# A planned attention and feed-forward kernel: single-row loads for batch 2, three more tiles transposed by DMA, and the sink values of later batches loaded already spread

## The chip, the cores and the metric

The kernel runs on one core of a Trainium2 chip. The metric is the device time of one execution in microseconds. Thirteen executions of the kernel before are on record; their median is 225.15 us. PE is the matrix engine, PEld its weight loads, DVE the vector engine, ACT the scalar engine, POOL the GpSimd engine and SP the engine that only issues DMAs and waits.

## The reference, cut to what matters

Attention with a window of 128 positions and four sink positions, for 4 batches, 8 heads, 768 positions and head width 64, is followed by a normalised two-layer feed-forward block with a residual.

```python
scores = scale * np.matmul(q, k.transpose(0, 1, 3, 2))
keep = is_sink | in_window            # key < 4, or 0 <= query - key < 128
a = softmax(np.where(keep, scores, -1e9))
attn = np.matmul(a, v)                # B, H, S, D
x = attn.transpose(0, 2, 1, 3).reshape(B, S, H * D)
xn = (x - mean) / np.sqrt(var + 1e-6) * g_ln
out = x + np.maximum(xn @ w_ch1, 0.0) @ w_ch2     # 512 -> 2048 -> 512
```

## The kernel before, in words

The 3072 positions are 24 tiles of 128, six to a batch: tile `t` is row block `r = t % 6` of batch `t // 6`. The tiles are collected into eight groups for the feed-forward part, of 2, 2, 2, 4, 4, 4, 4 and 2 tiles (`GROUPS`). So tiles 6 to 9 are group 3, and batch 2 is tiles 12 to 17.

The program is not written in its order. Each piece of work is an `Op` with the engines that may run it, an estimated duration on each, the pieces that it depends on, a key (its urgency) and the buffers that it takes or uses. `Plan.emit` walks a model of the engines, takes next what can start first (among nearly equal starts the lowest key), and emits the instructions in that order. It reserves PSUM itself: two double banks (`"pw"`, names `wide`) and four single banks (`"pm"`, names `single`). While the plan's clock stands under 26 us it also inserts filler matmuls on a constant tile (`spin`). On each engine the emitted order is final, so an instruction that has to wait holds up all that stand behind it on that engine. DMA queues count as engines in this: casting loads are issued from POOL, transposing DMAs and output stores from SP.

For one tile, `scores` multiplies q and k into double banks, ACT takes the exponential, and DVE or POOL clears what lies outside the window. `values` multiplies the result with v. Where it is `joined`, the values of tile `t - 1` are the first part of one PE piece with the scores of tile `t` and take two single banks; for the tiles of `ALONE` (6 to 9) the values are a PE piece of their own and take one double bank. `normalise` divides, takes mean and variance and centres the tile into a buffer `xn` (six of them), all on DVE. Then the tile has to be turned, with the model dimension on the partitions, into the buffer `xnt` of its group (three of those). Tiles from `DMA_TILE = 10` on are turned by a transposing DMA from SP (line 753). Tiles 0 to 9 are turned on PE by four transposes into a single bank (line 763) and copied out by DVE or ACT (line 766, which calls line 223 or 225).

The sinks are worked per batch in `sinks`. `mul_k` spreads the four sink keys, four small matmuls give the sink scores (line 534) and ACT takes their exponential. For the sink values, two matmuls with a selecting matrix copy the four sink rows of v to all partitions (`mm_v`, line 521), and two DVE multiplications with the mask `smask` keep those of each head (`mul_v`, line 527). In batches 1 to 3 `mm_v` takes a double bank.

`up` and `down` are the two matrix products of the feed-forward part (lines 787 and 827), with ACT or DVE taking the maximum with zero between them, and a DVE instruction and an SP store at the end of each tile. Their order is fixed by `mlp_order`: the three first groups all go up, then all go down, and from group 3 on each group goes up and then down. Attention of a tile has a key some 30 us of feed-forward work ahead of its group's place in that order, so the planner slips it in between.

Loads of batch 0, the weights, q and k of batch 1 and v of batch 1 are queued first, with at most seven casting loads outstanding. Then batch 2 is queued in one run: twelve loads of q and k, each of which is followed by a transposing DMA from SP (line 482), and later six of v. Batch 3 is queued row by row, each row once the scores of an earlier row of batch 2 have been taken.

Of the kernel before, what the change touches and what calls it, by code (L numbers as in the profile page):

```python
# [9 lines left out]
BF16 = mybir.dt.bfloat16  # L10
# [11 lines left out]
class Op:  # L22
    def __init__(self, engs, fn, deps, key, alloc, uses):
        self.engs, self.fn, self.key = engs, fn, key
        self.deps, self.alloc = [d for d in deps if d is not None], list(alloc)
        self.deps += [b.users[0] for b in uses if b.users]
        self.end = None
        for b in list(alloc) + list(uses):
            b.users.append(self)


# [132 lines left out]
def kernel(  # L164
# [12 lines left out]
    nc = tc.nc  # L177
# [16 lines left out]

    GROUPS = [2, 2, 2, 4, 4, 4, 4, 2]
    ALONE = (6, 7, 8, 9)
    NB0 = 3
# [51 lines left out]
    NEG_TILES = 3  # L249
    DMA_TILE = 10  # L250
    W2_FIRST = 3
# [71 lines left out]
    op({"POOL": 0.5}, const_sel, [begun], -499.4)  # L323
    sinks_done = op({"POOL": 0.9}, const_sinks, [begun], -440)


# [91 lines left out]
    def load_w(which, c, key, took=2.6):  # L418
# [8 lines left out]
        w_in[(which, c)] = load(0.85, took, go, key)  # L427


    prepped, kqb, turns = {}, {}, {}  # L430
# [67 lines left out]

    def sinks(b, key):

# [10 lines left out]

        vb = [Buf("pw", 0)] if b else [Buf("pm", 0), Buf("pm", 0)]

        def mm_v(_):
            if b:
                halves = [room_for(vb[0])[:, i] for i in range(2)]
            else:
                halves = [room_for(i) for i in vb]
            vb[0].t = halves
            for half in range(2):  # L520
                nc.tensor.matmul(halves[half][:, 0:4 * (D + 1)], lhsT=sel,
                                 rhs=vn_buf[b % 2][:, 0, 4 * half:4 * half + 4, 0:D + 1],
                                 start=True, stop=True, skip_group_check=True)

        def mul_v(_):
            for half in range(2):
                nc.vector.tensor_tensor(
                    vs[:, 4 * half:4 * half + 4], vb[0].t[half][:, 0:4 * (D + 1)].rearrange("p (h d) -> p h d", d=D + 1),
                    smask[:, 4 * half:4 * half + 4].unsqueeze(2).to_broadcast([128, 4, D + 1]), op=ALU.mult)

        def mm(_):
# [8 lines left out]

        o1 = op({"DVE": 0.2}, mul_k, ready(b, range(HP), 0, NS, 0, 0) + [sunk.get(b - 2), sinks_done, edone.get((RB * b, 0)) if b else None], key, (), [kb])
        ov = op({"PE": 0.22}, mm_v, [vcast[(b, 0)], sinks_done, ones_done] + ready(b, range(HP), 0, 0, 256, S), key, vb)
        vs_done[b] = op({"DVE": 0.8}, mul_v, [ov, vread.get((b - 2, RB - 1))], key, (), vb)
        o2 = op({"PE": 0.4}, mm, [o1] + ready(b, range(HP), 0, 0, 256, S), key, [pb], [kb])
        sunk[b] = op({"ACT": 0.6}, ex, [o2], key, [eb], [pb])

    ebuf = {}

    def scores(t, halves, key, lead=None):

# [13 lines left out]
        def mm(_):  # L564
            if lead:
                lead.fn(None)
            for pb, eb, part in zip(pbs, ebs, parts):
# [7 lines left out]
                for i, hp in enumerate([2 * half + i for half in part for i in range(2)]):  # L575
                    for h2 in range(2):
                        nc.tensor.matmul(pb.t[:, h2, i],  # L577
                                         lhsT=kb.t[64 * h2:64 * (h2 + 1), 1, hp, 128 * r:128 * (r + 1)],
                                         rhs=kb.t[64 * h2:64 * (h2 + 1), 0, hp, 128 * r:128 * r + n],
                                         start=not added, stop=True, skip_group_check=True)  # L580

        cost = 0.2 + 0.23 * n / 256 * len(halves) + (0.43 * len(halves) if added else 0.0)
        hps = [2 * half + i for half in halves for i in range(2)]
        deps = ready(b, hps, 128 * r, 128 * (r + 1), 128 * r, 128 * r + n) + [neg_done, edone.get((t - 1, 1)) if last else None]
        if lead:
            o0 = op({"PE": cost + lead.cost}, mm, deps + lead.deps, key, lead.alloc + pbs + ebs, [kb] + lead.uses)
            lead.rest(o0)
        else:
            o0 = op({"PE": cost}, mm, deps, key, pbs + ebs, [kb])

        for pb, eb, part in zip(pbs, ebs, parts):
# [25 lines left out]
            for half in part:  # L617
                edone[(t, half)] = o

    def weights_of(t, half, i, h2, lo):  # L620
# [6 lines left out]

    class Lead:
        pass

    def values(t, key, joined=False):

# [3 lines left out]
        vn, vs = vn_buf[b % 2], vs_buf[b % 2]  # L636
        banks = [Buf("pm", 0), Buf("pm", 0)] if joined else [Buf("pw", 0)]
        sums = []
# [9 lines left out]
        def mm(_):  # L648
            po = [room_for(i) for i in banks]
            po = po if joined else [po[0][:, i] for i in range(2)]  # L650
            sums[:] = [i[:, 0:4 * (D + 1)] for i in po]
# [30 lines left out]
        if joined:  # L682
            lead = Lead()
            lead.fn, lead.deps, lead.alloc, lead.uses, lead.cost = mm, deps, banks, uses, cost
            lead.rest = lambda o: normalise(t, key, o, banks, sums)
            return lead
        normalise(t, key, op({"PE": cost}, mm, deps, key, banks, uses), banks, sums)

    def normalise(t, key, o, banks, sums):
# [61 lines left out]

        if t >= DMA_TILE:
            o = op({"SP": 1.25}, lambda _: nc.sync.dma_start_transpose(room(), xnb[t].t), [o], key, alloc,
                   [xnb[t], xtb[g]])
            turned[t] = op({"XD": 0.4}, None, [o], key, (), [xnb[t], xtb[g]], 6.0 if t < 18 else 0.0)
            return
# [96 lines left out]
    def attention(t, key):  # L853

        alone = t - 1 in ALONE
        scores(t, (0, 1), key, None if alone or t == RB else values(t - 1, key, True))
        if alone:
            values(t - 1, key - 0.5)
        if t == NT - 1:
            values(t, key + 1.0)  # L860
# [27 lines left out]
    for r in range(RB):  # L888
        load_v(1, r, -430 + r)

    for b in range(B):
# [25 lines left out]
        if b == 1:  # L917
            for hp in range(HP):
                prep_runs(1, 0, hp, k0 - 12 + 3 * hp)
        else:  # L920

            for r in range(RB if b == 2 else 0):
                for x in range(2):
                    load_qk(b, x, r, k0 - 60 + r)
            for r in range(RB if b == 2 else 0):
                load_v(b, r, k0 - 50 + r, [prepped[(b, RB - 1, 1)]])
        for r in range(RB):
            if b == B - 2:

                t = RB * (b + 1) + r  # L930
                seen = [edone[(RB * b + r - 1, 0)]] if r else []
                for x in range(2):
                    load_qk(b + 1, x, r, akey(t) - 45, seen + [prepped[(b, RB - 1, 1)]])
                load_v(b + 1, r, akey(t) - 40, seen)
            attention(RB * b + r, akey(RB * b + r))
            if r == 1:
                sinks(b, akey(RB * b + 2) - 1)

# [53 lines left out]
```

## Time and profile before

| what | value |
|---|---|
| median of 13 executions | 225.15 us |
| shortest and longest of them | 224.54 and 1254.28 us |
| second longest | 225.8 us |
| the profiled execution | 1254.28 us |
| its span, first to last instruction | 1252.6 us |
| PE busy in that span | 1228.8 us |
| DVE, ACT, POOL busy | 116.0, 115.1, 85.6 us |

The profiled execution is the one that took 1254.28 us; the other twelve lie between 224.54 and 225.8 us. Its clock column shows 1.000 throughout, yet its matmuls are far too long for a time of 225 us. Durations on the other engines are those of single instructions and don't depend on PE. Read from the page, then, the order of all instructions, and the durations on DVE, ACT, POOL and the DMA queues; durations on PE have to be scaled before they can be set against 225.15 us.

### The profile page before, as it was taken

The page shows a single profiled execution, that of the slowest core. Times are in us where ns is not written, and L with a number is a line of the kernel's source. Part 1 is how long each engine was busy: PE and PEld are TensorE (multiplying, and loading weights), DVE is VectorE, ACT ScalarE, POOL GpSimd, SP SyncE. Part 2 cuts the span into 40 slices and gives each one's busy share as a digit, 9 for nine tenths or more (in the row PEclk, how much of TensorE's full clock was granted, in tenths as well). Part 3 has the DMA queues.
Part 4 walks back from the last instruction along what each step waited for, and adds up shares of the span by engine and source line. Part 5 has one row for each costly group of instructions (what it writes and reads, how often), then busy time and mean ns, then how long its engine had stood idle before and what let it go on. Part 6 is the DMA issues. An engine that isn't in the chain of part 4 may idle for free.

```text
span 1252.6 us, 4479 instructions
## 1 busy us (share of the span) xinstructions
PE 1228.8 (98%) x1805; PEld 427.3 (34%) x1826; DVE 116.0 (9%) x239; ACT 115.1 (9%) x159; POOL 85.6 (7%) x116
## 2 busy tenths in 40 slices
PE   9999999999999999999999999999999999999998
PEld 5445555623242322223332232322232322222433
DVE  1101000111110111111100100100000100000000
ACT  1211101110100111100011100011000011000000
POOL 5001040000030001010000000000000000000000
DMA  9024190001053004022100000000000000000000
GB/s 172 12 39 59 9 89 0 1 0 30 17 45 27 21 13 34 4 34 38 25 0 5 4 8 13 17 4 0 0 9 21 13 5 0 0 17 8 9 0 17
DMA packets 84774, 25.59 MB, mean 20 GB/s; under 512 B 74385, under 2 KB 81809, under 8 KB 84754
## 3 DMA queue, kind: packets, MB, share of 16 engines
q0 software_dynamic: 59392, 13.24, 12.0%
q1 hardware_dynamic: 24818, 11.67, 3.8%
q10 hardware_dynamic: 544, 0.39, 0.1%
q8 instruction: 14, 0.23, 0.1%
q14 instruction: 6, 0.05, 0.0%
HBM read 27.27 MB, written 6.29 MB: 27 GB/s over the span
## 4 chain that ended last, share of the span: by engine, by line
PE 98%; issue 2%; DVE 0%; DVEq 0%
PE single L787 40%; PE single L827 39%; PE wide L577 5%; PE single L237 2%; PE single L661 1%; PE wide L573 1%; PE wide L458 1%; PE single L458 1%; PE wide L661 1%; PE single L664 1%; PE single L763 1%; PE wide L664 1%; PE wide L644 1%; PE single L644 0%; PE single L867 0%
## 5 line engine op out<-in xcount | busy, mean ns | idle before, releaser
L787 PE MATMUL single<-xnt,w1s 128*128 128x256 bf16 (+1 forms) x505 | 505.1, 1363 | 6.6 <-issue 6.6
L827 PE MATMUL single<-w2s,h1t 128*128 128x512 bf16 x247 | 331.0, 1703 | 7.3 <-issue 7.3
L787 PEld LDWEIGHTS <-w1s 128*128 128x128 bf16 x512 | 157.6, 310 | 333.8 <-issue 333.2
L827 PE MATMUL single<-w2s,h1n 128*128 128x512 bf16 (+2 forms) x139 | 167.5, 1542 | 4.7 <-issue 4.7
L827 PEld LDWEIGHTS <-h1t 128*128 128x128 bf16 x256 | 78.2, 308 | 247.0 <-issue 247.0
L593 ACT ACTIVATE e<-wide 128x1024 bf16<-128x1024 f32 x44 | 45.0, 1024 | 371.1 <-PE wide L577 359.6
L827 PEld LDWEIGHTS <-h1n 128*128 128x128 bf16 x144 | 42.5, 303 | 104.6 <-issue 103.9
L840 DVE SCALAR_TENSOR_TENSOR ot<-single,rs,xt 128x512 f32<-128x512 f32 (+2 forms) x25 | 18.2, 729 | 542.5 <-PE single L827 523.2
L796 ACT ACTIVATE h1t<-single 128x512 bf16<-128x512 f32 x60 | 35.8, 597 | 327.9 <-PE single L787 312.1
L577 PE MATMUL wide<-qkt 64*128 64x256 bf16 (+1 forms) x192 | 62.9, 921 | 0.0
L605 POOL TENSOR_SCALAR_AFFINE_SELECT e<-e 128x512 bf16<-128x512 bf16 (+1 forms) x13 | 9.3, 716 | 662.3 <-ACT e L593 662.3
L661 PEld LDWEIGHTS <-e 128*128 128x128 bf16 x192 | 46.4, 254 | 22.0 <-issue 22.0
L664 PEld LDWEIGHTS <-e 128*128 128x128 bf16 x160 | 39.0, 249 | 16.8 <-issue 16.8
L796 ACT ACTIVATE h1n<-single 128x512 bf16<-128x512 f32 x30 | 17.9, 597 | 230.2 <-PE single L787 230.2
L661 PE MATMUL single<-vn,e 128*128 128x65 bf16 x104 | 35.4, 476 | 0.9 <-issue 0.9
L577 PEld LDWEIGHTS <-qkt 64*128 64x128 bf16 x192 | 18.8, 207 | 42.8 <-issue 42.5
L664 PE MATMUL single<-vn,e 128*128 128x65 bf16 x88 | 31.5, 471 | 0.0
L661 PE MATMUL wide<-vn,e 128*128 128x65 bf16 x88 | 31.2, 484 | 0.0
L458 PEld LDWEIGHTS <-qkn 128*64 128x64 bf16 x192 | 25.8, 305 | 6.4 <-issue 6.4
L664 PE MATMUL wide<-vn,e 128*128 128x65 bf16 x72 | 26.4, 465 | 0.0
L237 PE MATMUL single<-spinner 128*128 128x128 bf16 x68 | 23.6, 656 | 1.1 <-DVE spinner L263 1.1
L703 DVE RECIPROCAL rc<-single 128x4 f32<-128x4 f32 x26 | 4.7, 179 | 212.6 <-PE single L644 127.6
(71 smaller groups left out, 336.7 us busy)
## 6 DMA issues: line engine op xcount, KB each, us to landing
out_dram<-ot SPq DMA_DIRECT2D x23, 256.0 KB, 2.0
vn<-in_v_dram POOLq DMA_DIRECT2D x24, 128.0 KB, 4.5
w1s<-in_moe_w_ch_dram POOLq DMA_DIRECT2D x4, 512.0 KB, 11.2
w2s<-in_moe_w_ch_dram POOLq DMA_DIRECT2D x4, 512.0 KB, 7.6
qkn<-in_q_dram POOLq DMA_DIRECT2D x12, 128.0 KB, 4.7
qkn<-in_k_dram POOLq DMA_DIRECT2D x12, 128.0 KB, 4.7
qkn<-in_q_dram POOLq DMA_DIRECT2D x1, 768.0 KB, 7.0
qkn<-in_k_dram POOLq DMA_DIRECT2D x1, 768.0 KB, 9.9
```

Of the source, the lines that this page charges most:

```text
L237: nc.tensor.matmul(single[3][:, 0:128], lhsT=spinner, rhs=spinner, start=True, stop=True, skip_group_check=True)
L458: nc.tensor.transpose(pb.t[64 * h2:64 * (h2 + 1), x, 128 * r:128 * (r + 1)], src[:, c, 2 * hp + h2, r, :], ident)
L573: nc.tensor.matmul(pb.t[:, h2], lhsT=ident, rhs=neg, start=True, stop=False, skip_group_check=True)
L577: nc.tensor.matmul(pb.t[:, h2, i], lhsT=kb.t[64 * h2:64 * (h2 + 1), 1, hp, 128 * r:128 * (r + 1)], rhs=kb.t[64 * h2:64 * (h2 + 1), 0, hp, ...
L593: nc.scalar.activation(eb.t, pb.t, AF.Exp, scale=scale)
L644: nc.tensor.matmul(sums[half], lhsT=esb[b].t[rows, 128 * (r - 2):128 * (r - 1)], rhs=vs[rows, 4 * half:4 * half + 4, :].rearrange("p h d - ...
L661: nc.tensor.matmul(pv[:, hh, :], lhsT=weights_of(t, half, i, h2, 0), rhs=vn[:, r, h, 0:D + 1], start=fresh and hh == 0, stop=(r == 0), ski ...
L664: nc.tensor.matmul(pv[:, hh, :], lhsT=weights_of(t - 1, half, i, h2, 128), rhs=vn[:, r - 1, h, 0:D + 1], start=False, stop=not (joined and ...
L787: nc.tensor.matmul(pb.t[:, n * i:n * (i + 1)], lhsT=w1s[:, j, 128 * (h0 + i):128 * (h0 + i + 1)], rhs=xtb[g].t[:, j, 0:n], start=(j == 0), ...
L796: nc.scalar.activation(hb.t, pb.t, AF.Relu)
L827: nc.tensor.matmul(pb.t[:, 0:n], lhsT=hidden(g, ht, ti), rhs=w2s[:, ht, c0:c1], start=(ht == 0), stop=(ht == NH1 - 1))
L840: nc.vector.scalar_tensor_tensor(ob.t[:, 0:n], in0=pb.t[:, 0:n], scalar=rsb[g][:, ti:ti + 1], in1=xb[t].t.rearrange("p h d -> p (h d)")[:, ...
```

## The change

Five edits are made together.

1. `load_qk` and `load_v` of batch 2 are queued in the loop over the rows of batch 1, one row at a time, each after the scores of an earlier row, as those of batch 3 were already.
2. Tiles 6, 7 and 8 are turned by a transposing DMA instead of PE transposes and a copy. Tile 9 stays on PE.
3. In batches 1 to 3 the sink rows of v are no longer spread by `mm_v`. Four casting loads from POOL bring each of the four rows straight to 32 partitions, into a buffer taken from the `xn` pool, and one DVE multiplication over 128x512 replaces the two over 128x260. The column of ones in the second `vs` buffer is copied once at the start.
4. In batches 1 and 3 the sink scores become the last part of the PE piece of the scores of row 2. In batch 2 they stay a piece of their own.
5. The values of tiles 6 to 9 take two single banks instead of a double one, which splits the division into two halves on DVE.

```diff
+    JOINED = (1, 3)
...
-    DMA_TILE = 10
+    BY_DMA = [6, 7, 8] + list(range(10, NT))
...
+    sinks_done = op({"DVE": 0.1}, lambda _: nc.vector.tensor_copy(vs_buf[1][:, :, D], smask), [sinks_done], -90)
...
+    def load_first_v(b, key, deps=()):
+        fb = first_v[b] = Buf("xn", 6)
+        def go(_):
+            fb.t = xnpool.tile([128, DM], BF16, name="xn")
+            for i in range(NS):
+                src = v[b, :, i, :]
+                nc.gpsimd.dma_start(fb.t.rearrange("(g s) (h d) -> s g h d", s=NS, h=H)[i],
+                                    bass.AP(src.tensor, src.offset, [[0, 128 // NS]] + list(src.ap)))
+        first_in[b] = load(3.4, 0.9, go, key, deps, [fb])
...
-        vb = [Buf("pw", 0)] if b else [Buf("pm", 0), Buf("pm", 0)]
+        vb = [Buf("pm", 0), Buf("pm", 0)]
...
+        def pick_v(_):
+            nc.vector.tensor_tensor(vs[:, :, 0:D], first_v[b].t.rearrange("p (h d) -> p h d", h=H),
+                                    smask.unsqueeze(2).to_broadcast([128, H, D]), op=ALU.mult)
...
-        ov = op({"PE": 0.22}, mm_v, [vcast[(b, 0)], sinks_done, ones_done] + ready(b, range(HP), 0, 0, 256, S), key, vb)
-        vs_done[b] = op({"DVE": 0.8}, mul_v, [ov, vread.get((b - 2, RB - 1))], key, (), vb)
-        o2 = op({"PE": 0.4}, mm, [o1] + ready(b, range(HP), 0, 0, 256, S), key, [pb], [kb])
-        sunk[b] = op({"ACT": 0.6}, ex, [o2], key, [eb], [pb])
+        if b == 0:
+            ov = op({"PE": 0.22}, mm_v, [vcast[(b, 0)], sinks_done, ones_done] + ready(b, range(HP), 0, 0, 256, S), key, vb)
+            vs_done[b] = op({"DVE": 0.8}, mul_v, [ov], key, (), vb)
+        else:
+            vs_done[b] = op({"DVE": 0.6}, pick_v, [first_in[b], sinks_done, vread.get((b - 2, RB - 1))], key, (), [first_v[b]])
+        deps = [o1] + ready(b, range(HP), 0, 0, 256, S)
+        def rest(o2):
+            sunk[b] = op({"ACT": 0.6}, ex, [o2], key, [eb], [pb])
+        if joined:
+            return Joined(mm, deps, [pb], [kb], 0.32, rest)
+        rest(op({"PE": 0.4}, mm, deps, key, [pb], [kb]))
...
-        banks = [Buf("pm", 0), Buf("pm", 0)] if joined else [Buf("pw", 0)]
+        banks = [Buf("pm", 0), Buf("pm", 0)] if joined or narrow else [Buf("pw", 0)]
...
-        if t >= DMA_TILE:
+        if t in BY_DMA:
...
+        trail = None
+        if t % RB == 2:
+            if t // RB in JOINED:
+                trail = sinks(t // RB, key, True)
+            else:
+                sinks(t // RB, key - 1)
+        scores(t, (0, 1), key, None if alone or t == RB else values(t - 1, key, True), trail)
         if alone:
-            values(t - 1, key - 0.5)
+            values(t - 1, key - 0.5, narrow=True)
...
+    load_first_v(1, -424)
...
-        else:
-            for r in range(RB if b == 2 else 0):
-                for x in range(2):
-                    load_qk(b, x, r, k0 - 60 + r)
-            for r in range(RB if b == 2 else 0):
-                load_v(b, r, k0 - 50 + r, [prepped[(b, RB - 1, 1)]])
         for r in range(RB):
-            if b == B - 2:
+            if b < B - 1:
...
+                if r == 1:
+                    load_first_v(b + 1, akey(t) - 39)
             attention(RB * b + r, akey(RB * b + r))
-            if r == 1:
-                sinks(b, akey(RB * b + 2) - 1)
```

Since the planner chooses the order, each of these edits can move any other instruction of the program.

## The prediction

> **What bounds the kernel now.** I read the page's first table, then the chain that ended last, then the timeline of PE around tiles 6 to 9, the waits, and last the DMA issues.
>
> ```profile
> span 1252.6 us, 4479 instructions
> PE 1228.8 (98%) x1805; PEld 427.3 (34%) x1826; DVE 116.0 (9%) x239; ACT 115.1 (9%) x159; POOL 85.6 (7%) x116
> ...
> PE 98%; issue 2%; DVE 0%; DVEq 0%
> ```
>
> The chain is PE from end to end. But this execution took 1254.28 us and twelve others about 225, so its PE must be rescaled. In the chain's list of pieces, runs of 128x512 matmuls advance by 1.3225 us each:
>
> ```profile
> 271.88 5.29 PE single L827 x4
> ```
>
> The Trainium skill, "TensorE: Matmul & The Clock Gate", section "Wait — 56ns, not 53.3ns?", gives 215.7 ns for such a matmul on a warm array, 55.6 for 128 columns, and N/2.4 GHz plus 2.5 ns between. The trace disagrees by 1322.5/215.7 = 6.13 with a clock column of 1.000; the same page ("Seeing it yourself") warns that clock events can be unreliable. Divided by 6.13, PE's 1228.8 us are 200.5 us. The other twelve executions leave 225.15 minus the 1.68 us that this one has outside its span, 223.5 us. So PE streams for 90% of an ordinary execution and some 23 us are start, end and waits which this trace cannot show. DVE's 116.0 us are then half of the time, POOL's 85.6 us 38%: PE is the bound, but no longer without gaps.
>
> **Where the touched work stands.** PE's timeline, columns start, length, line, tile names, count:
>
> ```profile
> 283.41 1.80 PE L521 MATMUL wide<-vn,sel 128*128 128x260 bf16 x2
> 284.70 11.10 PE L827 MATMUL single<-w2s,h1n 128*128 128x512 bf16 x8
> ...
> 323.20 1.62 PE L763 MATMUL single<-ident,xn 128*128 128x128 bf16 x4
> 324.48 10.92 PE L827 MATMUL single<-w2s,h1n 128*128 128x512 bf16 x8
> ...
> 372.30 1.62 PE L763 MATMUL single<-ident,xn 128*128 128x128 bf16 x4
> ...
> 414.28 1.35 PE L787 MATMUL single<-xnt,w1s 128*128 128x512 bf16 x1
> ```
>
> Tiles 6 to 9 are worked between the `down` pieces of groups 0 to 2 (line 827); 414.28 is the first `up` of group 3, which needs all four. There is feed-forward work on both sides of every touched piece, so PE time taken away there should come off the end.
>
> **The change, part by part.** PE first.
> - Transposes: 323.20 to 324.48 is 1.28 us for four, so three tiles give 3.84 us here, 0.63 rescaled. By the skill's price 12 x 55.6 ns = 0.67.
> - `mm_v` of batches 1 to 3: 283.41 to 284.70 is 1.29 us for two, 3.87 for six, 0.63 rescaled. By price 6 x (260/2.4 + 2.5 = 110.8 ns) = 0.66.
> - Sink scores as the tail of a scores piece: the same four matmuls. Only a wait and a pipeline gap can go; the diff's own costs differ by 0.08 us for each of two, 0.16. Bounds: -0.3 (two gaps) to +0.5, if the scores now wait for `ks` or for the batch's last q row. I take -0.1.
>
> Sum on PE: -7.7 us on the profiled 1254.28, that is 1246.6; on the median -1.26 by the trace, -1.33 by the price. I take -1.35, and -1.45 with the joining.
>
> DVE: six multiplications of 424 ns go (2.5 us). Three `pick_v` over 128x512 come. Line 603 does twice the elements in 690 ns, line 724 the same number from two SBUF inputs in 750 ns; "VectorE: DVE Perf Modes", section "What auto-detection actually checks", asks step 1 of every 16-bit tensor for the doubled rate, and `smask` is broadcast with step 0. So 0.35 to 0.75, and I take 0.68 each, 2.0 in all. The half-wise division costs 2 x (179 + 425) = 1208 ns against 208 + 691 = 899, four times 0.31 = 1.2. The ones column adds 0.1; one copy out (tile 7, DVE, 0.42) goes, and two on ACT (0.586 each). DVE gains about 0.4 us, ACT loses 1.2: nothing on the end while DVE is half idle, but each division keeps its PE successors 0.3 us later.
>
> POOL: 12 more casting issues. `vn` issues take 881 to 978 ns for 1024 runs; these have 256 each, the weights' issue takes 771. So 0.77 to 0.95 each, 3.1 to 3.8 per batch in one block, 10 in all on an engine that is 62% idle. Queued behind batch 1's block are the first rows of batch 2; behind the later ones a row of q, k, v, a window mask of 1.28 us (or DVE takes the mask), and the scale of a group (`ve`, `rs`). The covers are the distance between a row's load and its tile.
>
> SP and the DMA queues: three more transposing DMAs, 1.19 us on SP and landing after 2.4 us (4.1 at most); batch 2's twelve are spread instead of bunched. Bunched, they fared as follows: the first line is from the view of line 482, all 24 transposes of q and k.
>
> ```profile
> DMA to landing us min/median/max: 2.4/2.5/9.0
> ```
>
> The second is from the DMA issues between 150 and 180 us, where seven ran among the loads; its last column is the median time to landing.
>
> ```profile
> qkt<-qkn SPq DMA_TRANSPOSE x7, 7.9
> ```
>
> "DMA: Bandwidth & Descriptors", section "DMA Transpose (X-bar)", lets SP or ACT issue such transposes; all are SP's here, so they stay one stream. Behind each on SP stand stores and later transposes. Whoever waits: `up` of group 3. The vector timeline ends tile 8's `xn` at 355.45; 414.28 is 58.8 us later, rescaled 9.6 us. A transposition takes 1.2 + 2.4 = 3.6 us, at worst 1.2 + 9.0 = 10.2. Tile 9, which stays on PE, has its `xn` at 386.0, 28.3 us or 4.6 rescaled ahead. So I cost edit 2 at nothing beyond its gain. Without the `down` work between, the 3.6 us would stand against 0.24 of transposes and 0.59 of copy on PE's path.
>
> Loads: bunching or spreading batch 2 moves no byte. In the first 31 us of the profile the DMA engines are full, but batch 2 was queued behind weights and batch 1, so what is spread delayed no one ahead of it. The extra rows of v are 128 KB a batch, one `vn` load (0.9 us of queue). Nothing either way; bounds -1 to +1 for fewer collisions or later rows.
>
> PSUM: the double banks lose four `values` and three `mm_v` and the scores have them to themselves; the single banks gain four pairs of 2 us. `down` holds one single bank at a time, so two are left over. Bounds -0.7 to +0.5; I take 0.
>
> **Sum:** 225.15 - 1.45 = 223.7 us.
>
> **Rivals.** A change of 0.2%, 0.45 us, is about what a measurement of this kernel can tell from none.
> 1. *More goes than streaming.* Each removed piece was also a place where in-order PE waited for DVE (`xn`, `vs`). At five such places, 0.1 to 0.25 us each: 222.4 to 223.2. For it: 23 us aren't streaming. Against it: those may all lie in the start, where the profile shows exponentials of 1.02 us and copies of 0.8 one after another.
> 2. *Nothing comes off.* If PE, in an ordinary execution, waits for masks and divisions among the `down` pieces, the 1.35 us turn into waiting, and the time is 224.8 to 225.5. Against it: in the waits, apart from the spinner's 1.1 us, PE waited for "issue" alone; but in an execution six times longer on PE that says little. The planner could also put the transposes of tiles 6 to 8 so late that the edit doesn't do what it says.
> 3. *The turned tile comes late.* SP takes its queue in order: tile 8's transpose stands behind those of batch 2's rows, each pair holding SP for 2.4 us and waiting for loads that land after 4.7 us (11.5 at most). It decides from 9.6 us after `xn`: two pairs (4.8), the wait for a load (4.7) and its own landing (3.6) make 13.1, so PE would stand 3.5 us before `up` of group 3, less the 1.45 gained: 227.2. A single pair makes it break even. The same form is open to `pick_v`, behind which DVE would wait for a load that the plan puts at 2.9 us after issue and the trace at 4.5. For it: the profile's 9.0 and 11.5. Against it: line 755 books 6.0 us extra for turning such a tile, so the planner leaves room.
>
> **Chances.** The forecast 0.50; rival 1 0.15; rival 2 0.13; rival 3, with other ill luck of a new order, 0.22. Faster by over 0.2%: 0.65; within: 0.13; slower: 0.22. The range: 222.4 (all of rival 1) to 226.4 (a late tile by 2.7 us), which leaves out the worst of rival 3, about 0.12, and a little below.
>
> **What would show it.** After: line 763 with 28 transposes instead of 40; line 521 twice only; seventeen `xnt<-xn` issues; twelve new issues from `v` on POOL, three of `pick_v` of 0.6 to 0.75 us; the transposes of tiles 6 to 8 landing under 4 us and over 5 us before group 3's first `up`. Rival 3 would show as PE waiting for a DMA ahead of that `up`, rival 2 as new waits for ACT or DVE with line 763 gone. If PE's busy sum falls by the price and the time rises, my claim that PE work here is never waited for is wrong.

## The result, and the profile after

| | before | after |
|---|---|---|
| median | 225.07 us (48 runs) | 229.27 us (11 runs) |
| shortest and longest | 224.44 and 1254.28 us (the next 225.81) | 227.39 and 230.31 us |
| ratio | | 1.0167 [1.0150, 1.0184] |
| the profiled execution, its span | 224.52, 222.8 us | 229.07, 227.3 us |

The forecast was 223.7 us and faster; the kernel became 1.7% slower. The columns of spans come from profiled executions at ordinary speed: that of before is the first experiment below, since the trace on which the prediction rested had PE stretched sixfold. Medians take in every execution of a run; ratios and their intervals leave out executions more than 1.5% above the fastest of the same kernel, so the two can differ.

The head of the page after, and the first line of its chain that ended last:

```profile
span 227.3 us, 4479 instructions
...
PE 216.0 (95%) x1787; PEld 123.1 (54%) x1808; DVE 117.7 (52%) x248; ACT 110.6 (49%) x156; POOL 88.5 (39%) x123
...
PE 85%; DVE 9%; issue 2%; DMA 2%; ACT 1%; DVEq 0%; ACTq 0%
```

The edits did what they say: 28 PE transposes instead of 40, `mm_v` in batch 0 alone, seventeen transposing DMAs for turned tiles, twelve new sink loads. PE is busy for 216.0 us, and was for 217.4 in the kernel before. That fall of 1.4 us is not a measure of the work taken off: some of the matmuls after ran at a lower clock (below), and the trace lacks some records of matmuls (39 fewer, where 18 were taken out). But PE's share fell to 95%. DVE's share of the chain, 9%, was 7% in the kernel before. The waits of PE after, columns total, times and longest in us, tell where:

```profile
PE single L819 <- DVE vs L553: 2.4, 1, 2.4
PE single L559 <- DVE mv L751: 1.6, 1, 1.6
```

Two single waits, ahead of an `up` (line 819) and ahead of the sink scores of batch 2 (line 559). Neither exists in the kernel before. The DVE instructions named there only happened to end at about the time; who is really waited for has to be found. PE's timeline after, columns start, length, line, tile names, count, idle time before:

```profile
77.41 2.76 PE L859 MATMUL single<-w2s,h1n 128*128 128x512 bf16 x11
82.59 4.33 PE L819 MATMUL single<-xnt,w1s 128*128 128x512 bf16 x12 [2.42 <-DVE vs L553]
...
87.65 1.90 PE L819 MATMUL single<-xnt,w1s 128*128 128x512 bf16 x8
91.12 0.40 PE L559 MATMUL single<-qkt,ks 128*32 128x512 bf16 x4 [1.57 <-DVE mv L751]
```

The `up` at 82.59 is the first of group 3, which needs tiles 6 to 9 turned. PE was done with the last `down` at 77.41 + 2.76 = 80.17 us. In the kernel before, PE came to the same twelve `up` matmuls without a gap (its line 787):

```profile
79.34 2.76 PE L787 MATMUL single<-xnt,w1s 128*128 128x512 bf16 x12
```

So follow tile 8. Its `xn` is the ninth on the vector timeline after:

```profile
67.84 1.02 DVE L756 SCALAR_TENSOR_TENSOR xn<-xt,mv,gb 128x512 bf16<-128x512 bf16 x1
```

It ends at 68.86 us. SP's timeline after, same columns:

```profile
68.44 1.21 SPq L785 DMA_TRANSPOSE xnt<-xn  x1
69.74 1.42 SPq L507 DMA_TRANSPOSE qkt<-qkn  x1
71.25 0.54 SPq L877 DMA_DIRECT2D out_dram<-ot  x1
71.89 1.24 SPq L507 DMA_TRANSPOSE qkt<-qkn  x1
73.22 0.54 SPq L877 DMA_DIRECT2D out_dram<-ot  x1
73.81 1.38 SPq L785 DMA_TRANSPOSE xnt<-xn  x1
75.28 10.44 SPq L507 DMA_TRANSPOSE qkt<-qkn  x3
```

The first line is tile 7's, the sixth is tile 8's: two row transposes and two stores stand between, SP has no pause, and tile 8 is taken 4.95 us after its `xn`. The view of that one DMA, in us:

```profile
DMA to landing us min/median/max: 8.7/8.7/8.7
```

The view counts from the start of the DMA's instruction on SP: 73.81 + 8.7 = 82.5, when PE goes on. The last line of SP's timeline holds the second gap. Its third transpose, of the last q row of batch 2, starts only when that row's load has landed (issued at 70.19, 14.3 us under way, 84.5). In a narrower window it has a line of its own, and the view of that one DMA follows:

```profile
84.53 1.19 SPq L507 DMA_TRANSPOSE qkt<-qkn  x1
...
DMA to landing us min/median/max: 6.3/6.3/6.3
```

So it lands at 90.9, and at 91.12 PE goes on with the sink scores.

A third loss hides in the timeline of PE: twelve `up` matmuls took 4.33 us after the gap. The view by windows of 5 us, whose first columns after the length are PE's busy time and count, and whose third number from the end is the granted clock:

```profile
80.00:85.00 5.00, 2.58 (x7) 0.87 (x7) 3.04 (x7) 0.51 (x1) 0.87 (x1) 0.74 1.80 129
85.00:90.00 5.00, 4.55 (x31) 1.97 (x29) 2.23 (x6) 3.59 (x6) 3.18 (x5) 0.92 2.27 155
```

The clock is 0.74 of full speed in the 5 us that hold the gap. Where there is no gap the same twelve take 2.75 us (`light_loads` below), so the dip costs 1.58. The account: 2.42 + 1.58 + 1.57 = 5.57 us lost, less the 1.45 that the prediction reckoned as saved, is an estimate of 4.1; the medians differ by 229.27 - 225.07 = 4.20, the two profiled executions by 4.55. So near an agreement is partly luck, since, as it seems, not every execution has the dip: of the changed kernel's twelve on record, the profiled one among them, four have a mean clock of 1.000 and took 227.39 to 228.27 us, the other eight have 0.985 to 0.998 and took 228.03 to 230.31.

Last, the DMA issues of 50 to 85 us, count and median us to landing:

```profile
qkn<-in_q_dram POOLq DMA_DIRECT2D x8, 128.0 KB, 8.2
...
qkt<-qkn SPq DMA_TRANSPOSE x11, 7.0
...
xnt<-xn SPq DMA_TRANSPOSE x3, 7.0
```

The prediction had seen such a line, seven transposes at 7.9 us, and taken 2.4.

### The profile page after: what moved, and what is told of

The parts are those of the page before. It is cut to its first block, busy times and chain, and to the rows that moved or that the text cites. A ratio compares the mean times of both kernels' runs of the same rounds, so it can differ in the third digit from the quotient of the medians.

```text
span 227.3 us, 4479 instructions
## 1 busy us (share of the span) xinstructions
PE 216.0 (95%) x1787; PEld 123.1 (54%) x1808; DVE 117.7 (52%) x248; ACT 110.6 (49%) x156; POOL 88.5 (39%) x123
## 4 chain that ended last, share of the span: by engine, by line
PE 85%; DVE 9%; issue 2%; DMA 2%; ACT 1%; DVEq 0%; ACTq 0%
PE single L859 35%; PE single L819 35%; PE wide L611 4%; DVE st L748 2%; PE single L696 2%; DVE xn L756 2%; DVE xt L742 2%; DMA xnt<-in_q_dram 2%; PE single L699 2%; PE wide L483 1%; PE wide L607 1%; PE single L679 1%; PE single L245 1%; PE single L483 1%; PE single L795 1%
## 5 line engine op out<-in xcount | busy, mean ns | idle before, releaser
L819 PE MATMUL single<-xnt,w1s 128*128 128x256 bf16 (+1 forms) x506 | 88.4, 329 | 2.7 <-DVE vs L553 2.4
L819 PEld LDWEIGHTS <-w1s 128*128 128x128 bf16 x512 | 49.0, 98 | 37.7 <-issue 7.2
L859 PE MATMUL single<-w2s,h1t 128*128 128x512 bf16 x247 | 55.8, 379 | 0.9 <-issue 0.6
L859 PEld LDWEIGHTS <-h1t 128*128 128x128 bf16 x256 | 24.5, 98 | 29.9 <-issue 0.9
L859 PE MATMUL single<-w2s,h1n 128*128 128x512 bf16 (+2 forms) x138 | 28.5, 355 | 0.6 <-issue 0.5
L418 POOL DMA_DIRECT2D vn<-in_v_dram x24 | 21.7, 905 | 6.6 <-DMA qkn<-in_q_dram 2.8
L859 PEld LDWEIGHTS <-h1n 128*128 128x128 bf16 x144 | 12.8, 98 | 13.3 <-issue 1.1
L756 DVE SCALAR_TENSOR_TENSOR xn<-xt,mv,gb 128x512 bf16<-128x512 bf16 x24 | 19.6, 818 | 0.6
L696 PEld LDWEIGHTS <-e 128*128 128x128 bf16 x192 | 13.1, 98 | 2.5 <-DVE ks L532 0.2
L611 PE MATMUL wide<-qkt 64*128 64x256 bf16 (+1 forms) x192 | 14.4, 262 | 0.0
L409 POOL DMA_DIRECT2D qkn<-in_q_dram x12 | 10.8, 904 | 2.4 <-DMA vn<-in_v_dram 1.6
## 6 DMA issues: line engine op xcount, KB each, us to landing
w2s<-in_moe_w_ch_dram POOLq DMA_DIRECT2D x4, 512.0 KB, 14.5
```

What stands on the lines that cost most here:

```text
L409: nc.gpsimd.dma_start(dst[:, r], (q, k)[x][b, :, 128 * r:128 * (r + 1), :].rearrange("h p d -> p h d"))
L418: nc.gpsimd.dma_start(vn_buf[b % 2][:, r, :, 0:D], v[b, :, 128 * r:128 * (r + 1), :].rearrange("h p d -> p h d"))
L611: nc.tensor.matmul(pb.t[:, h2, i], lhsT=kb.t[64 * h2:64 * (h2 + 1), 1, hp, 128 * r:128 * (r + 1)], rhs=kb.t[64 * h2:64 * (h2 + 1), 0, hp, ...
L696: nc.tensor.matmul(pv[:, hh, :], lhsT=weights_of(t, half, i, h2, 0), rhs=vn[:, r, h, 0:D + 1], start=fresh and hh == 0, stop=(r == 0), ski ...
L756: nc.vector.scalar_tensor_tensor(xnb[t].t, in0=xf, scalar=mvb[g][:, ti, 0:1], in1=gb, op0=ALU.subtract, op1=ALU.mult)
L819: nc.tensor.matmul(pb.t[:, n * i:n * (i + 1)], lhsT=w1s[:, j, 128 * (h0 + i):128 * (h0 + i + 1)], rhs=xtb[g].t[:, j, 0:n], start=(j == 0), ...
```

## The experiments

The theory that I began with: edit 2 is the whole loss, through transposes that land late. Its rivals were DVE, which is busy for 97% of 60 to 80 us, the new sink loads, and SP's order. Up to `light_loads` the expectations take tile 9's `xn` (73.23 us, ending near 74.0) for tile 8's, and so give SP's order too little weight; by a count of tiles on the vector timeline tile 8's ends at 68.86, and the runs from `early_turn` on follow from that. Ratios are to the kernel before, run beside each.

**before_again**: the kernel before, profiled once more.

> The kernel before, unchanged, to have its trace at the PE speed of its ordinary executions: about 225.1 us. Every theory: PE has no gap ahead of the first up piece of group 3 and none ahead of the sink scores of batch 2. If the late-tile theory is right, the transposing DMAs that run beside the down pieces of groups 0 to 2 land after well over the 2.4 us of the other trace, 6 us or more, because the queues are loaded. If DVE overload is the new thing, DVE is under 85% busy between tiles 6 and 9 here, against 97% in the changed kernel from 60 to 80 us.

It took 224.52 us, and its page has the line that the stretched trace could not give:

```profile
span 222.8 us, 4500 instructions
...
PE 217.4 (98%) x1826; PEld 123.8 (56%) x1826; DVE 115.1 (52%) x239; ACT 112.2 (50%) x159; POOL 84.1 (38%) x116
```

PE waits for the constant tile of the filler matmuls (1.1 us), `xn` (0.3) and a copy (0.2), and for nothing else. Tile 8's `xn` ends at 71.61, `up` of group 3 begins at 79.34. Late landings are not new: six of batch 2's row transposes, issued between 53 and 61 us among the row loads, took 7.1 to 9.3 us here too, but nothing of PE waited for them. The last ones, with those loads landed, took 2.5 to 2.6 us, two of them back to back, so these didn't hold one another up. And DVE was busy for 93% of 70 to 75 us without a gap on PE.

**no_dma678**: edit 2 undone.

```diff
-    BY_DMA = [6, 7, 8] + list(range(10, NT))
+    BY_DMA = list(range(10, NT))
```

> The changed kernel with tiles 6 to 8 turned on PE again (edit 2 undone). Late-tile theory: the 2.4 us gap ahead of group 3's first up piece goes, and with it the clock dip behind it (some 1.7 us), at a price of 0.67 us of transposes: 229.0 becomes 225.3 to 226. Late-q-row theory (1.6 us gap at the sink scores of batch 2 is what matters, and tile 8 would have waited on something else): 228.5 to 229.5. DVE-overload theory: the gap stays in another form, since the chain to the centred tile is as late as before: 228 or more.

224.77 us, 0.9997 [0.9982, 1.0013]; both gaps gone, though DVE was busy for 94% of 70 to 80 us. The loss belongs to edit 2, or to what it moves, and not to DVE's load. Run again to see whether the other edits pay:

> The changed kernel with edit 2 alone undone, a second time: the first gave a ratio of 0.9997 [0.998, 1.001]. Theory: the DMA-turned tiles are the whole loss, and the six matmuls of mm_v and the joined sink scores come off PE (0.66 + 0.1 us) with nothing else moved: 224.3 to 224.6 us, ratio 0.9966. Rival: the 0.76 us of PE turn into other waiting (a longer start, the divisions in two halves, POOL's sink loads): 224.9 to 225.3, ratio 0.9993 to 1.001.

224.56 us, 0.9988 [0.9975, 1.0002]. The centre lies between theory and rival; 0.3 us of the expected 0.76 showed. Neither nothing nor 0.5 us is excluded, but the theory's ratio of 0.9966 lies outside the intervals of both runs.

**nodma_wide**: edits 2 and 5 undone (the values of tiles 6 to 9 in a double bank).

> Edits 1, 3 and 4 alone: tiles 6 to 8 turned on PE and their values in a double bank, as before. If the division in two halves costs something (4 x 0.31 us on the vector engine, and a later xn each time), this is 0.3 to 0.8 us faster than the kernel with edit 2 alone undone, that is 223.9 to 224.5. If the single banks were worth having, it is slower than that by as much. If neither, both agree within 0.2 us.

225.36 us, 1.0006 [0.9987, 1.0026]: not faster, so nothing shows that the halved division holds back the saving. The interval is too wide for more.

**bunched**: edit 1 undone, batch 2's rows loaded in one run again.

> The changed kernel with batch 2's loads queued in one run as before (edit 1 undone; the spread sink row of batch 2 is still loaded). Late-q-row theory: the 1.6 us gap at the sink scores of batch 2 goes: 227 to 227.6. If spreading the loads is also what keeps the DMA queues loaded while tiles 6 to 8 are turned, the first gap shrinks as well and the time falls to 224 to 225.5. If the late tile alone decides: 228.5 to 229.5.

234.54 us, 1.0424 [1.0398, 1.045], worse than any theory had it. PE waits 4.9 us for `xnt` ahead of `up` and 2.5 for `qkt` ahead of the sink scores. SP has the row transposes of the whole batch in front: tile 8's `xn` ends at 70.10, but

```profile
76.04 2.67 SPq L507 DMA_TRANSPOSE qkt<-qkn  x2
78.76 3.48 SPq L785 DMA_TRANSPOSE xnt<-xn  x2
```

and the second of the two tiles, tile 8, is issued at 80.93, 10.8 us after its `xn`, and lands 8.1 us later, at 89.06. Here SP's order is the larger part.

**only_dma678**: the kernel before with edit 2 alone.

> The kernel before with tiles 6 to 8 turned by DMA and nothing else (edit 2 alone). In the kernel before the q and k loads of batch 2 have landed by 65 us and its transposes land in 2.5 us from 68 us on. Late-tile theory with loaded queues: tile 8 turns in quiet queues, no gap, 224.0 to 224.8. If edit 2 is bad by itself (a transposing DMA is in the wrong place on SP, or one more of them is too many): 226 to 229.

229.04 us, 1.0137 [1.0076, 1.0198]. In the profiled execution, at 232.1 us the longest of the four, PE waits 5.9 us for `xnt<-xn`. Again all three turned tiles stand behind the twelve rows, at 74.76 to 78.6 us, and land some 7.5 us later beside six loads of v.

**mmv**: edit 3 undone, no sink loads in batches 1 to 3.

> The changed kernel with the sink values of later batches spread by the two PE matmuls again and their twelve POOL loads gone (edit 3 undone). If those loads (0.6 us each on POOL, and their bytes in the queues) make the others late: 225.5 to 227. If they do nothing: 0.66 us more of PE, 229.3 to 229.9.

229.21 us, 1.0196 [1.0147, 1.0245]. PE waits 2.1 us for `xnt<-xn`; tile 8's `xn` ends at 66.87, SP takes it 7.1 us later, at 73.94, and it lands after 8.5 us. The sink loads are not the cause.

**long_runs**: each load of a row of q and k reads one run of 2 KB for each partition, and so other rows than the reference asks for.

> The changed kernel with every instruction in the same place on every engine; only the row loads of q and k for batches 2 and 3 read the same number of bytes as 128 runs of 2 KB instead of 1024 of 256 bytes, so the rows that they bring are other rows of q and k. If tile 8's turning DMA lands late because the queues are full of short packets: its landing falls from 8.7 us to under 5, the 2.4 us gap and the 1.6 us gap both go, 223.7 to 225. If it is late because SP reaches it late, or because transposing DMAs hold each other up: landing over 6 us, 228 to 229.5. If DVE overload decides: the same, 228 to 229.5.

228.6 us, 1.0096 [1.0062, 1.0129]. In the profiled execution, at 225.9 us the fastest of eleven, tile 8's transpose took 10.3 us to land, no less, and PE waited 1.9 us ahead of `up`. So it is not the number of packets in the loads of q and k alone; those of v were left as they are. The load of the last q row landed after 8.4 us instead of 14.3, and the gap ahead of the sink scores went.

**tile8_pe**: tile 8 back on PE, 6 and 7 turned by DMA.

> The changed kernel with tile 8 back on PE; 6 and 7 stay on DMA. If only the last of the turned tiles comes late: both gaps go, 224.2 to 225. If three extra transposing DMAs load the queues and delay the q rows of batch 2 all the same, or tile 7 is now the late one: 226 to 228.

227.09 us, 1.0109 [1.0044, 1.0174]. The gap ahead of `up` is gone, 2.1 us ahead of the sink scores stay. So the first gap is tile 8's own, and two added transposes still go with a late q row.

**lat12**: the planner books 11.0 us for a turned tile instead of 6.0.

> The changed kernel with the planner told that turned tiles 6 to 8 land 5 us later than it books now, near what the trace shows; the work is the same. If the loss is a planner that is too hopeful and has other work to put first: 224.5 to 226. If there is nothing left to put between (the down pieces of groups 0 to 2 are used up), the gap stays: 228 to 230.

230.64 us, 1.0255 [1.0218, 1.0292]. The planner puts `up` behind the sink scores, and PE waits 4.2 us for these instead. Time booked between is of use only where there is work to put there.

**light_loads**: every instruction in its place; the row loads of q, k and v of batches 2 and 3 bring an eighth of their bytes. Of the edit, the part for q and k:

```diff
-            nc.gpsimd.dma_start(dst[:, r], (q, k)[x][b, :, ...
+            nc.gpsimd.dma_start(dst[:, r, 0:1], (q, k)[x][b, 0:1, ...
```

> The changed kernel with every instruction where it stands there, but each load of a row of q, k and v of batches 2 and 3 brings one head of the eight (an eighth of its bytes and packets); the other seven keep older values, so these batches are not computed. Theory A, the turned tiles land late because their transposing DMAs share the DMA queues with the casting loads: tile 8's transpose lands within 2.4 to 4 us instead of 8.7, PE waits at neither place (ahead of group 3's up, 2.4 us after; ahead of batch 2's sink scores, 1.6 us after), and the time is 223.7 to 224.8 us. Theory B, transposing DMAs hold one another up or SP takes them late, whatever the loads do: landings of 6 us and more stay, both gaps stay, 228 to 229.5 us. Theory C, the vector engine at 97% makes tile 8's xn late and this alone is the matter: xn still ends near 74.0 us, and group 3's up still starts more than 2 us late.

223.54 us, 0.9941 [0.9922, 0.996]. Tile 8's `xn` ends at 69.09, SP takes it at 71.91, it lands 2.4 us later. The view of that DMA, then PE's timeline:

```profile
DMA to landing us min/median/max: 2.4/2.4/2.4
...
78.06 2.76 PE L859 MATMUL single<-w2s,h1n 128*128 128x512 bf16 x11
80.66 2.75 PE L819 MATMUL single<-xnt,w1s 128*128 128x512 bf16 x12
...
85.96 0.40 PE L559 MATMUL single<-qkt,ks 128*32 128x512 bf16 x4
```

No gap, and twelve matmuls in 2.75 us. With light loads the changed kernel is 1.34 us faster than the kernel before, near the 1.45 of the prediction; the kernel before was not run with light loads, so how much of the 1.34 is the change's own isn't shown. Theory A holds and C falls: `xn` was never late. On B this run is mixed, because SP's queue too moves faster with light loads (2.8 us instead of 4.95), and POOL is busy for 76.7 us instead of 88.5.

**early_turn**: SP's order alone; the transposes of tiles 6 to 8 are issued right behind their `xn`.

> The changed kernel with SP's queue alone in another order: the transposing DMAs of tiles 6, 7 and 8 stand right behind the xn that they turn, so tile 8's is moved ahead of one transpose of a q or k row and two stores, and tile 7's and 6's ahead of a row or two. In the changed kernel tile 8's xn ended at 68.86 us, SP took its transpose at 73.81, it landed 8.7 us later at 82.5, and up could have started at 80.2. Theory A, the delay is the sum of SP's order (4.95) and of the landing beside the loads (8.7): with 2.3 us less of the first, tile 8 is issued near 71.5 us and lands near 80.2; the gap ahead of up shrinks from 2.4 to 0 to 0.5 us, the one ahead of batch 2's sink scores stays at 1.6 to 2.5 (its row's load lands no earlier, and its own transpose stands one place later), and the time is 226.2 to 227.8 us. Theory B, the queues alone set when a transpose lands and SP's order doesn't matter: what is issued earlier lands as late, up waits 2 us or more, 228.5 to 229.5 us.

230.48 us, 1.0171 [1.0098, 1.0243]. The gap ahead of `up` is gone, as theory A said: tile 8's transpose is issued at 71.05 and lands 7.0 us later, at 78.1. But PE's timeline shows what followed:

```profile
80.62 2.75 PE L819 MATMUL single<-xnt,w1s 128*128 128x512 bf16 x12
...
90.69 0.40 PE L559 MATMUL single<-qkt,ks 128*32 128x512 bf16 x4 [4.69 <-DMA qkt<-qkn]
```

The last q row comes no earlier (its transpose is issued at 84.1 and takes 6.3 us), and PE waits 4.7 us for it. Theory A's mechanism held for the first gap and its time was a miss: with the first gap gone the second takes all of it.

**later_b3b**: what else is in the queues by then. The order of POOL differs between the kernel with edit 2 undone and the changed one. Of the first:

```profile
75.77 1.04 POOL L770 TENSOR_TENSOR rs<-ve,neg_half 128x4 f32<-128x4 f32 x1
83.90 1.11 POOL L641 TENSOR_SCALAR_AFFINE_SELECT e<-e 128x512 bf16<-128x512 bf16 x1 [7.09 <-PE single L819]
...
86.73 0.97 POOL L409 DMA_DIRECT2D qkn<-in_q_dram  x1
```

and of the changed kernel:

```profile
74.16 1.04 POOL L770 TENSOR_TENSOR rs<-ve,neg_half 128x4 f32<-128x4 f32 x1
75.17 0.97 POOL L409 DMA_DIRECT2D qkn<-in_q_dram  x1
```

There POOL waits 7.09 us before it can mask, and batch 3's loads stand behind that mask. After the change the mask has gone to DVE, and batch 3's loads start 11.6 us earlier, into the queues on which batch 2's last rows are still under way. (In the kernel before they start at 80.78, and batch 2's row loads of q and k have all landed by 67.6.) In this run POOL reads a column of tile 13's exponentials before the first of them; PE and ACT keep their order, and so does DVE up to batch 3's `pick_v`, past 100 us.

```diff
+            after is None or nc.gpsimd.tensor_copy(small.tile([128, 4], FP32, name="ve")[:, 0:1], after.t[:, 0, 0, 0:1])
```

> The changed kernel with the order of PE, DVE and ACT unchanged; POOL reads one column of the exponentials of tile 13 before the first load of batch 3, so that those loads start near 85 us instead of at 75.2. Theory A, the queues are congested by batch 3's rows: the last q row's load and tile 8's transpose land within 5 us, PE waits at neither place, 223.7 to 225.2 us. Theory B, the backlog is batch 2's own loads and the added transposes: tile 8's transpose still lands after 7 us or more, the load of batch 2's last q row after 12 us or more, both gaps stay, and the time is 228 to 229.5 us.

225.46 us, 1.0036 [1.0018, 1.0053]: against the kernel before the loss falls from 4.2 us to 0.6. PE's timeline in the profiled execution, at 224.07 us the fastest of fourteen:

```profile
80.58 2.75 PE L819 MATMUL single<-xnt,w1s 128*128 128x512 bf16 x12
...
86.11 0.40 PE L559 MATMUL single<-qkt,ks 128*32 128x512 bf16 x4 [0.16 <-issue]
```

Each theory was half right. The time is near A's. But batch 2's last row loads still land after 14.5 to 15 us, as B said; they were queued ahead of batch 3's. What batch 3's rows had held up is the last q row's transpose: issued at 83.4, it now lands after 2.4 us instead of 6.3. Tile 8's landing fell from 8.7 to 7.3 us only, and SP took it after 3.1 us instead of 4.95; it landed at 80.45, just in time.

**early_laterb**: both together.

> Both together: SP takes the transposes of tiles 6 to 8 right behind their xn, and batch 3's rows wait for tile 13's exponentials. Theory A of the run before: no gap ahead of up nor ahead of the sink scores, 223.5 to 224.8 us, faster than the kernel before by 0.1 to 0.6%. Theory B: no gap ahead of up, but the 4.7 us ahead of batch 2's sink scores stay, 228.5 to 230.5 us.

224.82 us, 0.9999 [0.9982, 1.0017]. No gap is left in the profiled execution, but executions range from 223.73 to 226.88: the shortest lies 0.7 us under the shortest of the kernel before, half of the forecast gain, and the medians don't differ.

**only_earlyb**: the kernel before with edit 2, and SP's order as in `early_turn`.

> The kernel before with edit 2 alone, and the transposes of tiles 6 to 8 right behind their xn in SP's queue (alone, without this, it took 229.0 us, its tiles standing behind all twelve rows of batch 2). Theory A, SP's order is the matter when the rows are bunched: tile 8's transpose is issued within 2 us of its xn (71.8 us) and lands before up (79.3 us), no wait of PE ahead of up, 224.0 to 225.2 us. Theory B, whatever the order, a transpose beside the loads lands after 7 us and more and the rows that it is put ahead of come late: 226.5 us or more.

231.24 us in the median, four runs of 226.33 to 232.86, ratio 1.0139 [1.0049, 1.023]. Theory A missed, and the time is B's. In the profiled execution, the one of 226.33, tile 8 is still taken 4.65 us after its `xn`, behind three transposes of rows and a store, and lands 5.2 us later, 2.4 us too late for `up`.

**two_tiles**: `early_laterb` with tile 8 back on PE.

> The changed kernel with tile 8 turned on PE, the transposes of tiles 6 and 7 right behind their xn in SP's queue, and batch 3's rows held back until tile 13's exponentials. PE saves 0.44 (two tiles) + 0.66 (mm_v) + 0.1. Theory A, what kept the mended kernel (224.8 us) from its saving is that tile 8's landing and the last q row have no margin left, so that some executions wait: with two transposes less beside the loads there is margin, and the time is 223.9 to 224.4 us, faster than the kernel before by 0.2 to 0.5%. Theory B, the work taken off PE turns into other waiting in any case: 224.7 to 225.2 us.

224.33 us, 0.9961 [0.9944, 0.9979], executions of 223.44 to 224.65. Its page:

```profile
PE 214.7 (96%) x1791; PEld 123.0 (55%) x1812; DVE 117.5 (53%) x246; ACT 111.3 (50%) x158; POOL 89.1 (40%) x125
```

This beats both kernels, before by 0.4%. It is the time of theory A, and not that of B, by which all the saved work turns into other waits; the margin itself, execution by execution, was not measured.

## Why the prediction was wrong

*PE is the bound, and work taken from it comes off the end*: right in part. `light_loads` gained 1.34 us against 1.45 forecast, `two_tiles` 0.7 of some 1.2 with two tiles turned; but with edit 2 undone and no gap left, only 0.2 and 0.3 us of 0.76 came off. The rescaled 200.5 us of PE were too few: `before_again` has PE busy for 217.4 of 222.8 us, so 5.4 us were start, end and waits, not 23, and the ground of rival 1 goes with them. And PE's busy time fell while the time rose, which the prediction had named as the end of its claim that PE work here is never waited for. The claim was wrong: in this stretch PE does wait, for DMAs, and the price of its work counts only where it doesn't.

*The transposition costs 1.2 + 2.4 = 3.6 us, "so I cost edit 2 at nothing beyond its gain"*: this step failed. From the end of `xn` to landing tile 8 took 4.95 us until SP got to it and 8.7 from there to landing, 13.65 us. The cover was larger than estimated, 80.17 - 68.86 = 11.3 us instead of 9.6, and still 2.3 too small. (In the kernel before it is 79.34 - 71.61 = 7.7 us: rescaling the stretched trace didn't give it either.) The sum has a slip besides: the view's 2.4 counts from the start of SP's instruction, so the 1.2 on SP is in it already, and a transpose in quiet queues costs 2.4 us in all. The worst case that the prediction wrote beside it, 1.2 + 9.0 = 10.2, left out SP's order; rival 3, which had it, left out the landing. Each alone would have been covered; `early_turn` takes away 3.0 us of the one (1.95 left) and 1.7 of the other, `light_loads` 2.1 and 6.3, and either closes the first gap.

*Rival 3, "The turned tile comes late"* came true, at 13.65 us where it had put 13.1, and was given 0.22. It had said that PE would then wait for a DMA ahead of that `up`; in the changed kernel the wait bears the name of a DVE instruction, in `mmv` and `bunched`, at the same place, that of `xnt<-xn`. Its sum was made of other terms: not two pairs of transposes and a wait for a load, but two transposes, two stores and the tail of tile 7's, without a pause; and 8.7 us of landing where it put 3.6. So the mechanism was rightly named, and the nearness of 13.1 to 13.65 is luck. Its argument against itself, that the planner books 6.0 us for turning such a tile, did not hold against 13.65, and `lat12` shows that booking 11.0 doesn't help either.

*Durations on the DMA queues "don't depend on PE"*: the assumption behind the choice of 2.4 over 9.0. An execution with PE six times slower spreads the same loads over six times the time. Its page and that of `before_again` show the busy share of the DMA engines in tenths, for 40 slices of each span:

```profile
DMA  9024190001053004022100000000000000000000
...
DMA  7999999999999599999999102311011232012102
```

The first line is the stretched execution: its DMA engines are idle for most of the span. In the second, at ordinary speed, they are busy in nearly all of the first 22 slices, some 122 us. The median landing of 2.4 to 2.5 us is that of quiet queues; the lines with 7.9 and 9.0, in which transposes ran among loads, were the ones that resembled an ordinary execution.

*Loads: "Nothing either way; bounds -1 to +1"*: failed too. Batch 3's rows start 11.6 us earlier than with edit 2 undone, since a mask changed its engine, and the transpose of batch 2's last q row landed late for it. `later_b3b` prices this at about 3.6 us, by closing the second gap and just closing the first. The prediction had listed "or DVE takes the mask" and had not asked what stood behind that mask on POOL.

*DVE "nothing on the end"*: right; no run shows PE held up by it, though it was busy for 94 to 97% of some stretches. `pick_v` took 0.69 us, forecast 0.68. The sink loads cost POOL 0.57 us each, not 0.77 to 0.95, and in `mmv` the time without them is the same within the intervals. *PSUM 0*: nothing in any trace speaks against it.

What stays open: why batch 2's last row loads take 11 to 15 us in the changed kernel and its two mended versions, but 4 to 7 with edit 2 undone and 5 to 10 in `mmv`. The three added transposes alone don't explain it, as `mmv` has them; nor does DVE's load, which was 94% where they took 4 to 7. The size of the packets has a part in it, by the 8.4 us in `long_runs`. Open too is where some 0.5 us of the other edits' saving goes: `no_dma678` and `no_dma678_b` show 0.2 and 0.3 of 0.76, `two_tiles` 0.7 of 1.2.

## What to carry to other kernels

Price a DMA from its issuing engine's queue to its landing, in a stretch of the trace where the same traffic runs beside it, and add the two waits before holding them against the cover. If work leaves an in-order engine, look at what was queued behind it: loads that start sooner can be what makes the next transfer late. And when a first gap is mended and the time stays, look for the second one that was behind it, before the theory is given up.

## What the runs showed of the hardware

A transposing DMA of a 128x512 tile landed after 2.4 to 3.0 us beside light loads (tiles 6 to 8 in `light_loads`) and after 6.9 to 8.7 beside 128 KB casting loads (the same tiles in the changed kernel); in `long_runs` one took 10.3. The Trainium skill, "DMA: Bandwidth & Descriptors", section "Queues, rings and completion order", says that each DMA engine takes packets from its queues in turn; that agrees with a transpose that is slowed by loads on another queue, though no run here shows the turns themselves.

In the changed kernel the 5 us that hold a gap of 2.42 us on PE show a granted clock of 0.74, and the next 5 us 0.92; the dip made the gap dearer by two thirds. A gap of 2.14 us in `mmv` went with 0.78. But behind gaps of 2.38 us in `only_earlyb`, 2.05 in `tile8_pe` and 1.88 in `long_runs` the matmuls ran on at full speed: four took 1.02 us, eleven 2.76 and twelve 2.75. "TensorE: Matmul & The Clock Gate", section "What's actually happening", ties the drop to an idle window of about 3.4 us. In these traces gaps of 2.14 and 2.42 us were enough, and one of 2.38 was not, so the length of a gap alone does not tell whether the clock drops.
